# Local attention, then a squared-ReLU layer: four tiles to a group for the last eight tiles, and a new instruction order

## The chip, the cores and the metric

The kernel runs on one core of one Trainium2 chip. The metric is the device time in microseconds (us) of one execution; a number given for a version is the median of its runs. The profile is that of one execution, and its span is a little shorter than the device time.

## The reference

```python
scores = scale * np.matmul(q, k.transpose(0, 1, 3, 2))      # q, k, v: 4 x 8 x 768 x 64, float32
keep = is_global | is_local        # the first 8 keys, and the last 96 keys up to the query
scores = np.where(keep, scores + bias, -1000000000.0)       # bias: -slope of the head * distance
a = softmax(scores)
x = np.matmul(a, v)                # as 3072 tokens x 512
h = x @ w_in                       # 512 x 2048
r = np.maximum(h, 0.0)
out = (r * r) @ w_out              # 2048 x 512, float32
```

Each query sees at most 96 keys behind it and 8 at the start of its sequence. Most of the arithmetic is in the two products of the layer that follows.

## The kernel before

**Tiles.** The 3072 tokens are 24 tiles of 128, six to a sequence. Matmul inputs are bfloat16, sums float32.

**Attention of a tile.** GpSimd's queue (POOL) loads q, k and v, three DMAs a tile (line 213), converting them to bfloat16. q and k go into a ring of buffers (`qk_ring`, six for the first tiles and `NQ` = 3 for the later ones), v has a buffer for each tile. From tile 6 on, a DMA transpose on the SP queue (line 424) turns q and k into `qkT`. TensorE makes the scores (`sc`, line 487), ACT the exponentials (`exp`, line 553), DVE multiplies by mask and bias (`mul`, line 578), TensorE multiplies by v (`pv`, into the tile `po`, line 640), and DVE divides by the sum (`norm`, lines 667 and 668), giving `x`. From tile 8 on a DMA transpose (line 727) makes `xT` of it; before that TensorE does (`trx`, line 703). A score step may be joined to that of the tile before (`JOIN`), and then needs both tiles' `qkT`.

**The two products.** Two tiles form a block, 256 tokens. The first product `s1` (line 755) runs in eight units a block: each unit takes 256 of the 2048 hidden columns and is eight matmuls of 256 columns into one PSUM bank `hT` (128 x 512 float32). ACT applies the ReLU into `hr` (line 776), DVE squares it into `hs` (line 788), a ring of 14 buffers. The second product `s2` (line 828) takes `hs` as weights: two matmuls of 512 columns for each unit and tile, adding up over the eight units in `acc`, one PSUM bank for each tile of the block. ACT or DVE copies a finished bank to `o` (lines 328 and 330), and SP stores it (line 870). The last tile's sum is made in two pieces, of 384 and of 128 columns, the 128-column piece last.

**PSUM.** Eight banks: two for `acc`, six (tag `g`) shared by `hT`, `sc`, `po` and the transposes. An operation that takes a bank waits for the users of the bank's last tile.

**The order.** No engine picks its own order. A planner (`Plan`) gets each operation with a cost, its dependencies and a due time (`key`), plays the engines through, and always takes the operation with the smallest start plus a small multiple of its due time. The kernel then emits the instructions in that order, and each engine runs its own in order. `SHIFT` and `LEADS` move due times, `STEP` and `HOLD` tie a score step to a first-product unit, `SAFE` and `SAFEX` add a margin behind single transposes. `gate` is a small DVE write that holds back an early load.

Of the kernel before, what the change touches and what calls it, by code (L numbers as in the profile page):

```python
# [21 lines left out]
class Plan:  # L22
# [11 lines left out]
    SHIFT = {'T': 47, 'sc': -5.25, 'pv': -2, 'norm': 26.5, 'trx': -2, 'xT': 51, 'gk': 42, 'gv': -127.5, 'mul': 24, 'kl': 38.5, 'relu': 25.5, 'sq': 30, 's2': -5, 'o': 61, 'st': 78, ('mul', 3): 28, ('tr', 4): 10, ('xT', 5): -22, ('sc', 6): 14, ('pv', 7): -4, ('norm', 7): -17, ('trx', 7): -3, ('sc', 8): -12, ('pv', 8): -18, ('pv', 10): 45, ('sc', 11): 12, ('pv', 12): -50, ('sc', 13): 17, ('sc', 14): 6, ('pv', 14): 10, ('norm', 14): -28, ('sc', 15): -21, ('exp', 15): 20, ('exp', 16): 83, ('mul', 16): 92, ('norm', 16): -9, ('sc', 17): 32, ('pv', 17): 28, ('pv', 21): 9.5, ('pv', 22): -10, ('norm', 22): 8, ('s1', 2): -8.5, ('sq', 2): -10, ('relu', 3): 24, ('sq', 3): -82, ('s1', 5): 6, ('s1', 6): 30, ('sq', 6): 6, ('s1', 7): -6, ('sq', 7): -92, ('relu', 8): 40, ('s1', 9): -2, ('s1', 10): -10, ('s2', 0): 7.5, ('s2', 2): 1, ('s2', 4): -15, ('s2', 5): 37, ('s2', 6): -5, ('s2', 7): -3, ('s2', 9): 4.5, ('s2', 11): 30}  # L34
# [70 lines left out]
def kernel(  # L105
# [31 lines left out]
    NBLK = NT // 2  # L137
# [7 lines left out]
    NQ, NKT = 3, 2 * TPB  # L145
# [14 lines left out]
    v_sb = [const([P, H, VROW], BF16, f"v_{j}")[:, :, : D + 1] for j in range(NT)]  # L160
# [17 lines left out]
    LEADS = {3: 51, 4: 17, 5: 16, 6: 27, 8: 2, 9: 20, 10: 42, 11: 47, 12: 0, 14: 0, 15: 7.5, 16: 34, 17: 46, 20: 28, 21: 15, 23: 56}  # L178
# [6 lines left out]
    COPY = [14, 15, 19, 20, 22]  # L185
    BEHIND = {}
    HOLD = ((10, 0),)
    STEP = {(4, 0): -7, (12, 0): 37, (5, 0): -2, (10, 0): 29, (13, 0): 30, (23, 1): 81}
    JGATE = 11
    NHS = 14  # L190
    NWARM = 8
    NLATE, NO = 2, 4
    CUT = 3 * d_model // 4
    HALVES = ((NBLK - 3, 1), (NBLK - 2, 0), (NBLK - 2, 1))
# [9 lines left out]
    def slot(j):  # L204

        return j if j < NFIRST + 2 else NFIRST + 2 + j % NQ
# [14 lines left out]
    for j in range(NPLAIN):  # L221
        for n, src in ((0, q), (1, k)):
            t_ = const([P, d_model], FP32, f"plain_{n}{j}")
            nc.sync.dma_start(
                out=t_.rearrange("p (h d) -> p h d", h=H),
                in_=src_rows(src, j).rearrange("h p d -> p h d"),
            )
            plain[n, j] = t_
            land["qk"[n], j] = 4.1 + 1.1 * n
# [73 lines left out]
    for g in range(NFIRST + 2, NT, 6):  # L303
        js = range(g, min(g + 6, NT))
        o = plan.op(
            ("ones", g), {"DVE": 0.2}, lambda e, js=js: emit_ones(e, js),
            key=-1.0, ready=15.0,
        )
        ones.update({j: o for j in js})
# [41 lines left out]
    qk_users = [[] for _ in qk_ring]  # L351
    xT_op = {}
# [5 lines left out]
    for j in range(NT):  # L358
        b, t = divmod(j, TPB)
        first = t == 0  # L360
        need = 8 * (j // 2)
        base = need - LEADS.get(j, LEAD) + 4 * (j % 2)
# [4 lines left out]
        if j in late:  # L367
# [3 lines left out]
            if NFIRST + 2 + NQ - 1 <= j < JGATE:  # L371
# [10 lines left out]
                deps=qk_users[slot(j)] + [ones[j], gate], key=base, ready=issue[0],  # L382
            )
            qk_users[slot(j)] = []
            ld = plan.op(("data", j), {"DMAQ": 2.7}, None, deps=[ld])
# [36 lines left out]
        if j >= JQK:  # L422
            def emit_dT(e, j=j, T_=T_):
# [7 lines left out]
                deps=[land["q", j], land["k", j], xT_op[j - 3]] + ku, key=base - 6,  # L431
# [195 lines left out]
        for hf in range(2):  # L627
# [32 lines left out]
            users.append(p_)  # L660

# [21 lines left out]
        if 1 <= t < TPB - 1:  # L683
# [5 lines left out]
            )  # L689


        blk, tt = divmod(j, 2)
        if tt == 0:
            xT_users = []
        xT_ring = ("xT", 3, [xT_users]) if tt == 0 else None
        if j < JX:
# [16 lines left out]
            def emit_xT(e, j=j, blk=blk, tt=tt):  # L713
                if tt == 0:
                    tiles["xT", blk] = work.tile([P, KM, 2 * P], BF16, name="xT", tag="xT", bufs=3)
                any_copy(
                    e, tiles["xT", blk][:, :, tt * P : (tt + 1) * P], tiles.pop(("trx", j))
                )
# [4 lines left out]
        else:  # L723
            def emit_xT(e, j=j, blk=blk, tt=tt):
                if tt == 0:
                    tiles["xT", blk] = work.tile([P, KM, 2 * P], BF16, name="xT", tag="xT", bufs=3)
                nc.sync.dma_start_transpose(
                    out=tiles["xT", blk][:, :, tt * P : (tt + 1) * P],
                    in_=tiles["x", j].rearrange("p h d -> p (h d)"),
                )  # L730
# [9 lines left out]
        xT_of[blk] = xT_users  # L740
        if tt == 1:
            (xop if j >= JX else c)["deps"].append(xT_op[j - 1])


    order1 = [(blk, s) for blk in range(NBLK) for s in range(NSTEP)]
    square = {}
    s1_ops = {}
    for n, (blk, s) in enumerate(order1):
        users = []

        def emit_s1(e, blk=blk, s=s):
            hT = ps_g.tile([P, 2, 2 * P], FP32, name="hT", tag="g")
            for c in range(2):
                for kt in range(KM):
                    nc.tensor.matmul(  # L755
                        out=hT[:, c, :],
                        lhsT=w_in_sb[s][:, kt, c * P : (c + 1) * P],
                        rhs=tiles["xT", blk][:, kt, :],
                        start=(kt == 0),
                        stop=(kt == KM - 1),  # L760
                        skip_group_check=True,
                    )
            tiles["hT", blk, s] = hT

        a = plan.op(
            ("s1", blk, s), {"PE": 0.87}, emit_s1,
            deps=[xT_op[2 * blk], xT_op[2 * blk + 1], land["win", s]],
            key=float(n), takes=(*G, [users]),
        )
        s1_ops[blk, s] = a  # L770
        xT_of[blk].append(a)
        users.append(a)

        def emit_relu(e, blk=blk, s=s):
            hr = work.tile([P, 2, 2 * P], FP32, name="hr", tag="hr")
            nc.scalar.activation(hr, tiles.pop(("hT", blk, s)), Act.Relu)  # L776
            tiles["hr", blk, s] = hr

        rusers = []
        r = plan.op(("relu", blk, s), {"ACT": 0.48}, emit_relu, deps=[a], key=n + 0.5, takes=("hr", 2, [rusers]))  # L780
        users.append(r)
        rusers.append(r)
        husers = []

        def emit_sq(e, blk=blk, s=s):
            hs = work.tile([P, 2, 2 * P], BF16, name="hs", tag="hs", bufs=NHS)
            hr = tiles.pop(("hr", blk, s))
            nc.vector.tensor_mul(hs, hr, hr)  # L788
            tiles["hs", blk, s] = hs

        d = plan.op(("sq", blk, s), vec(0.61), emit_sq, deps=[r], key=n + 1.0, takes=("hs", NHS, [husers]))
        rusers.append(d)
        husers.append(d)
        square[blk, s] = (d, husers)

    for o in plan.ops:
        if o["name"][0] == "sc":
            j = o["name"][1]
            n = STEP.get(o["name"][1:], 4 * j - LEAD)
            if n >= 0 and j >= NFIRST:  # L800
                o["deps"].append(s1_ops[n // NSTEP, n % NSTEP])
                if o["name"][1:] in HOLD:
                    n += 1
                    s1_ops[n // NSTEP, n % NSTEP]["deps"].append(o)

    for blk in range(NBLK):
        last = blk == NBLK - 1
        acc_users = {}

        parts = [(0, None), (1, 0), (1, 1)] if last else [(0, None), (1, None)]  # L810
        order2 = (
            [(s, *p) for p in parts for s in range(NSTEP)]
            if last
            else [(s, *p) for s in range(NSTEP) for p in parts]
        )
        for s, sub, half in order2:
# [5 lines left out]
            def emit_s2(e, blk=blk, s=s, sub=sub, half=half, w=w, cols=cols, own=own):  # L822
                if s == 0:
                    pool, tag = (ps_g, "g") if own else (ps_acc, "acc")
                    tiles["acc", blk, sub, half] = pool.tile([P, w], FP32, name="acc", tag=tag)
                hs = tiles["hs", blk, s]
                for c in range(2):
                    nc.tensor.matmul(  # L828
                        out=tiles["acc", blk, sub, half],
                        lhsT=hs[:, c, sub * P : (sub + 1) * P],  # L830
                        rhs=w_out_sb[s][:, c, cols],
                        start=(s == 0 and c == 0),
                        stop=(s == NSTEP - 1 and c == 1),
# [3 lines left out]
            d, husers = square[blk, s]  # L837
            o = plan.op(
                ("s2", blk, s, sub), {"PE": 0.43 * w / d_model}, emit_s2,
                deps=[d, land["wout", s]] + users[-1:],  # L840
                key=8 * blk + s + 2.0 + (0 if not last else 8 * sub + 8 * (half or 0)),
# [4 lines left out]
            n = NSTEP * blk + s  # L846
            m = n + max([d for at, d in BEHIND.items() if n >= at], default=0)
            if m > n and m < NSTEP * NBLK:
                o["deps"].append(s1_ops[m // NSTEP, m % NSTEP])
            if s == NSTEP - 1:  # L850
# [70 lines left out]
```

## Time and profile before

| | us |
|---|---|
| device time, median of 3 runs | 211.02 (210.82 to 211.27) |
| span of the profile | 209.2 |
| TensorE (PE) busy | 202.4 |
| VectorE (DVE) busy | 141.4 |
| ScalarE (ACT) busy | 120.4 |
| GpSimd (POOL) busy | 74.0 |
| first product, 768 matmuls, busy | 93.3 |
| second product, busy | 87.1 |

PE is the matmul row and PEld the weight loads, which run beside the matmuls. The mean duration of a matmul in the groups (273 ns for 256 columns) includes its way through the array; when matmuls follow each other their starts are closer than that, so counts and stretches tell more than means. Some matmul records are missing from the trace, which looks like a short gap. The chain of waits goes back from the last instruction to what released each step.

### The profile page before, as it was taken

Reading aid. Unit: us, or ns where it says so; the run is one execution under the profiler, and the core shown is the slowest. Engines: PE = TensorE matmul, PEld = TensorE weight load, DVE = VectorE, ACT = ScalarE, POOL = GpSimd, SP = SyncE. Lnnn points to the kernel's source line nnn. Section 1 sums busy time; section 2 is a strip of 40 time slices with the busy share of each in tenths; the row PEclk is TensorE's granted clock in tenths of the full one; section 3 lists DMA queues with packets and bytes.
Section 4 is the critical chain, followed back from the end, with each engine's and each line's share of the span. In section 5 each row is a group of like instructions: output and inputs, shape, how many; then the busy total and the mean of one; then the engine's idle time right before and its main releaser. Section 6 shows DMA issues by size and latency. Waiting matters only on the chain.

```text
span 209.2 us, 4979 instructions
## 1 busy us (share of the span) xinstructions
PE 202.4 (97%) x1957; PEld 142.0 (68%) x1984; DVE 141.4 (68%) x370; ACT 120.4 (58%) x224; POOL 74.0 (35%) x91
## 2 busy tenths in 40 slices
PE   7989999999999999999999999999999999999994
PEld 3768887665756667676856676676676865865853
DVE  7698788533695788584958666676696865781730
ACT  6777688234872674655736564663575826841631
POOL 8997765541936086040545223122500000000000
PEclk9999999999999999999999999999999999999999
DMA  8999999999999999969799993979993421140402
GB/s 127 152 173 188 182 191 199 178 196 220 125 164 123 235 131 131 198 89 141 169 157 107 198 103 53 143 124 120 207 64 75 130 48 28 58 92 3 102 0 100
DMA packets 112664, 27.32 MB, mean 131 GB/s; under 512 B 103297, under 2 KB 109697, under 8 KB 112641
## 3 DMA queue, kind: packets, MB, share of 16 engines
q0 software_dynamic: 79200, 13.37, 84.8%
q1 hardware_dynamic: 33440, 13.64, 33.1%
q8 instruction: 15, 0.25, 0.5%
q14 instruction: 9, 0.07, 0.1%
HBM read 27.26 MB, written 6.29 MB: 160 GB/s over the span
## 4 chain that ended last, share of the span: by engine, by line
PE 88%; POOL 5%; DMA 3%; issue 1%; ACT 0%; POOLq 0%
PE acc L828 39%; PE hT L755 39%; PE sc L487 5%; PE po L640 4%; DMA win<-in_moe_w_in_dram 3%; POOL qk L213 3%; POOL v L213 2%; POOL win L213 1%; PE trx L703 1%; PE tr L400 1%; POOL pbi L267 0%; ACT o L328 0%; POOLq L267 0%; POOLq L902 0%
## 5 line engine op out<-in xcount | busy, mean ns | idle before, releaser
L755 PE MATMUL hT<-xT,win 128*128 128x256 bf16 x768 | 93.3, 273 | 0.7 <-DMA win<-in_moe_w_in_dram 0.6
L828 PE MATMUL acc<-wout,hs 128*128 128x512 bf16 (+2 forms) x373 | 87.1, 370 | 1.7 <-issue 0.3
L776 ACT ACTIVATE hr<-hT 128x512 f32<-128x512 f32 x96 | 57.4, 602 | 47.3 <-PE hT L755 41.5
L755 PEld LDWEIGHTS <-win 128*128 128x128 bf16 x768 | 72.9, 98 | 14.9 <-DMA win<-in_moe_w_in_dram 1.1
L788 DVE TENSOR_TENSOR hs<-hr 128x512 bf16<-128x512 f32 x96 | 64.8, 686 | 22.6 <-ACT hr L776 21.8
L828 PEld LDWEIGHTS <-hs 128*128 128x128 bf16 x400 | 36.8, 98 | 33.8
L553 ACT ACTIVATE esc<-sc 128x512 bf16<-128x512 f32 x78 | 39.9, 611 | 12.7 <-PE sc L487 12.6
L213 POOL DMA_DIRECT2D qk<-in_q_dram x23 | 20.7, 898 | 72.0 <-DMA qkT<-qk 55.9
L578 DVE TENSOR_TENSOR at<-esc,E 128x512 bf16<-128x512 bf16 x78 | 32.5, 424 | 10.3 <-ACT esc L553 7.5
L328 ACT COPY o<-acc 128x512 f32<-128x512 f32 (+2 forms) x21 | 11.6, 575 | 19.8 <-PE acc L828 19.8
L213 POOL DMA_DIRECT2D v<-in_v_dram x24 | 21.7, 904 | 1.4 <-DMA win<-in_moe_w_in_dram 1.0
L668 DVE TENSOR_TENSOR x<-po,rs 128x256 bf16<-128x256 f32 x48 | 20.4, 425 | 1.7
L213 POOL DMA_DIRECT2D qk<-in_k_dram x23 | 20.6, 895 | 0.5 <-DMA win<-in_moe_w_in_dram 0.5
L640 PEld LDWEIGHTS <-at 128*128 128x128 bf16 x352 | 15.7, 98 | 4.5
L640 PE MATMUL po<-v,at 128*128 128x65 bf16 x352 | 17.3, 193 | 0.0
L667 DVE RECIPROCAL rs<-po 128x4 f32<-128x4 f32 x48 | 8.5, 178 | 11.2 <-PE po L640 10.7
L487 PEld LDWEIGHTS <-qkT 64*128 64x128 bf16 x312 | 9.4, 94 | 5.9 <-issue 4.9
L487 PE MATMUL sc<-qkT 64*128 64x128 bf16 x192 | 12.6, 218 | 0.0
L487 PE MATMUL sc<-qkT,qkT 64*128 64x128 bf16 x120 | 8.5, 216 | 0.2 <-DVE rs L667 0.2
L330 DVE COPY o<-acc 128x512 f32<-128x512 f32 x4 | 2.8, 692 | 6.0 <-PE acc L828 6.0
L213 POOL DMA_DIRECT2D win<-in_moe_w_in_dram x8 | 6.1, 767 | 1.2 <-DMA win<-in_moe_w_in_dram 0.5
L213 POOL DMA_DIRECT2D wout<-in_moe_w_out_dram x8 | 5.7, 710 | 1.9 <-DMA win<-in_moe_w_in_dram 1.5
(45 smaller groups left out, 70.2 us busy)
## 6 DMA issues: line engine op xcount, KB each, us to landing
out_dram<-o SPq DMA_DIRECT2D x20, 256.0 KB, 3.2
v<-in_v_dram POOLq DMA_DIRECT2D x24, 128.0 KB, 5.8
qk<-in_q_dram POOLq DMA_DIRECT2D x23, 128.0 KB, 4.6
qk<-in_k_dram POOLq DMA_DIRECT2D x23, 128.0 KB, 5.2
win<-in_moe_w_in_dram POOLq DMA_DIRECT2D x8, 256.0 KB, 7.8
wout<-in_moe_w_out_dram POOLq DMA_DIRECT2D x8, 256.0 KB, 9.2
out_dram<-o SPq DMA_DIRECT2D x6, 128.0 KB, 2.4
qkT<-qk SPq DMA_TRANSPOSE x18, 4.8
```

Source lines behind the costliest of these rows:

```text
L213: nc.gpsimd.dma_start(out=dst, in_=src)
L328: nc.scalar.copy(dst, src)
L487: nc.tensor.matmul(out=tiles["sc", j, odd, g][:, at, :], lhsT=left[j - 1][half, pair, :] if kt else qkT[j % NKT][half, 1, pair, :], rhs=qk ...
L553: nc.scalar.activation(out=esc, in_=tiles.pop(("sc", j, odd, g)).rearrange("p a c -> p (a c)"), func=Act.Exp, scale=scale,)
L578: nc.vector.tensor_mul(at, tiles.pop(("esc", j, odd, g)), bias)
L640: nc.tensor.matmul(out=po[:, hi, :], lhsT=tiles["at", j, odd, g][:, at * P : (at + 1) * P], rhs=v_sb[kj][:, h, :], start=(i == 0), stop=(i ...
L667: nc.vector.reciprocal(rs, po[:, :, D : D + 1])
L668: nc.vector.tensor_tensor(out=x[:, 4 * hf : 4 * hf + 4, :], in0=po[:, :, :D], in1=rs.to_broadcast([P, 4, D]), op=Alu.mult,)
L755: nc.tensor.matmul(out=hT[:, c, :], lhsT=w_in_sb[s][:, kt, c * P : (c + 1) * P], rhs=tiles["xT", blk][:, kt, :], start=(kt == 0), stop=(kt ...
L776: nc.scalar.activation(hr, tiles.pop(("hT", blk, s)), Act.Relu)
L788: nc.vector.tensor_mul(hs, hr, hr)
L828: nc.tensor.matmul(out=tiles["acc", blk, sub, half], lhsT=hs[:, c, sub * P : (sub + 1) * P], rhs=w_out_sb[s][:, c, cols], start=(s == 0 an ...
```

## The change

Tiles 16 to 23 are worked in two groups of four tiles, 512 tokens, in place of four blocks of two. A first-product unit of such a group takes 128 hidden columns and is four matmuls of 512 columns into the same bank; there are 16 units. With two `acc` banks, the second product of a group makes two passes over the hidden columns: tiles 0 and 1 of the group, then tiles 2 and 3. In the last group the last tile is again cut into 384 and 128 columns. The purpose is fewer and wider matmuls and fewer weight loads in the first product.

Around it: `hs` becomes a ring of eight larger buffers, four units each; `xT` buffers hold four tiles; v gets a ring of 12 buffers, so that a load waits for the last reader of the tile 12 before; the q/k ring has four late buffers; six `o` buffers, the first two lent to the plain q and k of tile 0; `HOLD`, `STEP`, `LEADS` and `SHIFT` are new throughout, from a search over orders.

```diff
-    NBLK = NT // 2
+    QUADS = 16
+    GROUPS = [(j, 2) for j in range(0, QUADS, 2)] + [(j, 4) for j in range(QUADS, NT, 4)]
...
-    NQ, NKT = 3, 2 * TPB
+    NQ, NKT, NV = 4, 2 * TPB, 12
...
-    v_sb = [const([P, H, VROW], BF16, f"v_{j}")[:, :, : D + 1] for j in range(NT)]
+    v_ring = [const([P, H, VROW], BF16, f"v_{j}")[:, :, : D + 1] for j in range(NV)]
+    v_sb = {j: v_ring[j % NV] for j in range(NT)}
...
-    COPY = [14, 15, 19, 20, 22]
-    BEHIND = {}
-    HOLD = ((10, 0),)
-    STEP = {(4, 0): -7, (12, 0): 37, (5, 0): -2, (10, 0): 29, (13, 0): 30, (23, 1): 81}
+    COPY = sorted(j - 1 for j, _ in JOIN if j % TPB)
+    HOLD = ((15, 1), (17, 0), (19, 0))
+    STEP = {(14, 0): 36, (15, 1): 53, (17, 0): 46, (19, 0): 58, (20, 1): 62, (23, 1): 79, (4, 0): -7, (7, 0): 5, (13, 0): 32}
...
-    NHS = 14
+    NHS = 8
...
-    NLATE, NO = 2, 4
+    NLATE, NO = 2, 6
...
-                deps=qk_users[slot(j)] + [ones[j], gate], key=base, ready=issue[0],
+                deps=qk_users[slot(j)] + v_users[j % NV] + [ones.get(j % NV), gate], key=base, ready=issue[0],
...
-                deps=[land["q", j], land["k", j], xT_op[j - 3]] + ku, key=base - 6,
+                deps=[land["q", j], land["k", j], xT_op[j - (3 if j < QUADS - 2 else 6)]] + ku, key=base - 6,
...
-            hT = ps_g.tile([P, 2, 2 * P], FP32, name="hT", tag="g")
-            for c in range(2):
-                for kt in range(KM):
-                    nc.tensor.matmul(
-                        out=hT[:, c, :],
-                        lhsT=w_in_sb[s][:, kt, c * P : (c + 1) * P],
-                        rhs=tiles["xT", blk][:, kt, :],
...
+                hT = ps_g.tile([P, 4 * P], FP32, name="hT", tag="g")
+                nch = 4 // nt
+                for c in range(nch):
+                    ch = nch * s + c
+                    for kt in range(KM):
+                        nc.tensor.matmul(
+                            out=hT[:, c * nt * P : (c + 1) * nt * P],
+                            lhsT=w_in_sb[ch // 2][:, kt, (ch % 2) * P : (ch % 2 + 1) * P],
+                            rhs=tiles["xT", g][:, kt, :],
...
+        if nt == 4:
+            parts = [(2, None), (3, 0), (3, 1)] if last else [(2, None), (3, None)]
+            order2 = [(s, sub, None, n0 + 8.0 + s / 2) for s in range(nstep) for sub in (0, 1)]
+            if last:
+                order2 += [
+                    (s, sub, half, n0 + 16.0 + 8 * i + s / 2)
+                    for i, (sub, half) in enumerate(parts) for s in range(nstep)
+                ]
+            else:
+                order2 += [(s, sub, None, n0 + 16.0 + s / 2) for s in range(nstep) for sub in (2, 3)]
```

## The prediction

> **What bounds the kernel now.** I read the page's busy lines first, then the chain that ended last, then TensorE's waits, then the chain in order of time at both ends.
>
> ```profile
> span 209.2 us, 4979 instructions
> PE 202.4 (97%) x1957; PEld 142.0 (68%) x1984; DVE 141.4 (68%) x370; ACT 120.4 (58%) x224; POOL 74.0 (35%) x91
> PEclk9999999999999999999999999999999999999999
> DMA  8999999999999999969799993979993421140402
> ...
> PE 88%; POOL 5%; DMA 3%; issue 1%; ACT 0%; POOLq 0%
> ```
>
> TensorE is busy 97% at full clock, and 88% of the chain is TensorE; the other engines are far off. The second thing to see is the DMA line: nines until about 80 us and again around 105 to 125 us. Data arrives just in time, so DMA is the next bound behind TensorE. Does TensorE ever wait?
>
> ```profile
> PE warm L273 <- DVE zero L261: 1.2, 1, 1.2
> PE hT L755 <- DMA win<-in_moe_w_in_dram: 0.6, 2, 0.4
> PE acc L828 <- issue: 0.3, 2, 0.2
> PE acc L828 <- DVE hs L788: 0.3, 2, 0.2
> PE sc L487 <- DVE rs L667: 0.2, 1, 0.2
> ```
>
> Hardly: 2.6 us in all, most of it before the first product starts. The chain in order of time shows the two ends (start, us, what):
>
> ```profile
> 12.52 7.23 DMA win<-in_moe_w_in_dram
> 19.80 1.92 PE hT L755 x16
> ...
> 186.40 6.04 PE acc L828 x28
> 192.44 6.99 PE hT L755 x64
> ...
> 199.48 6.91 PE acc L828 x47
> 206.38 0.02 issue
> 206.41 0.27 ACT o L328
> ```
>
> Until 19.8 us the input weights set the pace; from 19.8 to 206.4 us TensorE has one piece after the other; then comes a tail of 2.8 us (evict, store, end). So only three things can move the time: the sum of TensorE's work after 19.8 us, new waits in it, and the tail.
>
> **What the Trainium skill says.** "TensorE: Matmul & The Clock Gate", section "Wait — 56ns, not 53.3ns?": a warm matmul starts every N/2.4 ns plus a fixed 2.5 ns or so, N being the columns. The trace agrees: 6.99 us / 64 = 109.2 ns for 256 columns (256/2.4 = 106.7), and 6.04 / 28 = 215.7 ns for 512 (213.3). The same page's "Back-to-back issue gap" gives 131 ns a matmul as a sustained rate at 512 columns; this trace does not agree, so I use 215.7. "DMA: Bandwidth & Descriptors", section "Issuing engines are not separate DMA queues": DMAs issued from different engines share the same 16 DMA engines and interleave. In the trace loads from POOL, transposes and stores from SP fall in the same nines.
>
> **Part 1: 512 columns a matmul (tiles 16 to 23).** 8 of 24 tiles change, so 256 of the 768 first-product matmuls become 128 of twice the width. Removed: 256 x 109.2 = 27.96 us. Added: 128 x 215.7 = 27.61 us. Gain 0.35 us, all on the path. It is that small because only the fixed 2.5 ns of 128 matmuls goes; the array streams the same columns. The 128 weight loads removed (98 ns each) overlap the matmuls (weight loads fill 68%) and cost nothing either way. Relu, square, evictions and second-product matmuls keep count and size.
>
> **Part 2: second product in two passes, groups of four.** The built program shows the order of each engine, which the planner sets. In TensorE's new order the 16 first-product units of a group stand in a row, then tiles 0 and 1 of the group accumulate, then 2 and 3. Can ACT and DVE keep up with 16 units? The stretch of 8 units at the end of before shows it:
>
> ```profile
> 192.44:199.42 6.98, 6.98 (x64) 6.20 (x64) 5.05 (x8) 4.37 (x8) 0.00 (x0) 1.00 0.35 76
> ```
>
> The columns are PE, weight loads, DVE, ACT and POOL. DVE needs 5.05 and ACT 4.37 us of 6.98, so both drain faster than TensorE fills, and 16 units behave like 8. I added up the trace's durations along the new order, without waits (an estimate): from the end of a first-product unit to the first second-product matmul that needs it there are now at least 3.6 us; in before the smallest distance was 1.7 us and cost nothing. So these waits have more room than before. Cost 0.
>
> **Part 3: the order, and what it asks of DMA.** Everything before the fourth first-product unit (19.8 us) is the same set of work behind the same weight load, so the start stays. After that attention runs earlier, because a group of four needs its four tiles whole. By the same sum, the scores of tile 13 come due at about 90 us (96.6 in before), of 14 at 97 (108.6), 17 at 119 (134.4), 19 at 134 (149.9), 22 at 163 (174.0). The loads must follow, through a DMA already at nines. Against that, the q/k ring goes from three slots to four, the gate before tile 8's load goes, and stores move back.
>
> The tight spots. (a) Tile 8 is now loaded before tile 7, which its scores need first (tile 7's stand joined with tile 6's, due at 53.1 us). A load takes POOL 3 x 0.9 = 2.7 us (0.898, 0.895 and 0.904 us an issue); tile 7's transpose landed at 49.3 us in before, so now near 52: 1 us of room. (b) The first product of tiles 8 and 9 is due at 76.8 us (80.1); tile 9's pv ends at 70.3, norm 2 x (0.18 + 0.43) = 1.2, the transpose's issue 1.2, landing 2.3 to 4.1 us later: 75.0 to 76.8, 0 to 2 us of room. (c) Tile 13's transpose waits on SP behind tile 10's (about 80 us) and lands near 87, due at 90. All hold, none with much to spare. What stands behind a late one: SP and TensorE are in order, so later transposes wait too, and every TensorE instruction after it slips by the full delay. I take 0.05 us for all this and keep 0 to 2 us.
>
> The v ring of 12 makes a load wait for the pv step 11 tiles back, tens of us before: 0. Fewer ones-memsets (12 x 65 ns) and one more kl copy (0.28 + 0.27 us) lie on a DVE that is 68% busy: 0.
>
> **Part 4: the tail.** In before the last accumulation is 128 columns wide; in the new order the 128-column piece goes ahead of the third tile's, and the last is the 384-column piece. TensorE's sum is the same, but what follows is longer: copy 0.48 against 0.27 us (ACT's timeline), store 1.9 against 1.6 us to landing (the DMA issues; KB, us).
>
> ```profile
> 205.51 0.48 ACT L328 COPY o<-acc 128x384 f32<-128x384 f32 x1 [2.01 <-PE acc L828]
> 206.41 0.27 ACT L328 COPY o<-acc 128x128 f32<-128x128 f32 x1 [0.41 <-PE acc L828]
> ```
>
> ```profile
> out_dram<-o SPq DMA_DIRECT2D x1, 192.0 KB, 1.9
> out_dram<-o SPq DMA_DIRECT2D x1, 64.0 KB, 1.6
> ```
>
> That costs 0.21 + 0.3 = 0.5 us, hidden by nothing. The third tile's first matmul also needs tile 0's bank: 0.22 + 16 x 0.056 + 0.17 = 1.3 us of room for 0.28 + 0.59 + 0.2 = 1.1: holds.
>
> **Sum.** 211.02 - 0.35 + 0.5 + 0.05 = 211.2 us. The change leaves the bound where it is, takes 0.35 us off it, and gives that back at the end.
>
> **Rivals.** (1) A transfer comes late and TensorE gains a wait. For it: DMA at nines, attention 12 to 16 us earlier in the middle, the three spots. Against it: one more ring slot, fewer stores ahead, and every spot holds in my sums. One or two late transfers of 0.5 to 1 us: 211.8 to 212.7, say 212.0 us. (2) The new order is smoother than I price it and the tail costs less: the waits of 0.3 + 0.3 us on the second product go, the 0.35 comes off, half the tail penalty is hidden: 211.02 - 0.35 - 0.6 + 0.25 = 210.3 us, faster. Against it: TensorE was saturated, so there is next to nothing left to gain, and some of those small waits are gaps where a matmul record is missing. (3) ACT or DVE falls behind in the two long first-product stretches, by 0.05 us on each of 32 units: 1.6 us, 212.8 us. The stage table above speaks against it.
>
> **From this to the numbers.** No difference 0.48 (211.2); a late transfer 0.30 and a slow engine 0.05, together slower 0.35; faster 0.17. The threshold of 0.2% is 0.42 us. The range runs from rival 2 with a margin less (210.4) to two late transfers of 1 us each (213.0).
>
> **What would show it.** In the changed kernel's profile: 128 matmuls of hT at 128x512 of about 216 ns each when back to back; TensorE's chain unbroken from 19.8 us to about 206.1; the last ACT copy 128x384 at 0.48 us, 2.8 + 0.5 us between TensorE's end and the span's end. A wait of TensorE for qkT or xT of over 0.4 us, near 53, 77 or 90 us, would show rival 1; a chain that ends near 205.4 us would show rival 2. I am wrong in the mechanism if the 512-column matmuls take clearly less than 216 ns.

## The result, and the profile after

The changed kernel takes 213.82 us (median of 6 executions, 212.86 to 214.14), the kernel before 211.17 us beside it (6 executions): 2.65 us slower, ratio 1.0115 with a 95% interval of 1.009 to 1.014. The prediction was 211.2 us; the time lies beyond its range of 210.4 to 213.0. A later series gave 214.43 against 211.68 us, 2.75 us slower. Medians from here on leave out executions in a slower state of the chip, those over 1.5% above the fastest of the same kernel.

The page of the changed kernel, the lines that were shown of before:

```profile
span 212.1 us, 4750 instructions
PE 203.2 (96%) x1832; PEld 128.8 (61%) x1856; DVE 142.0 (67%) x360; ACT 121.1 (57%) x223; POOL 73.8 (35%) x91
PEclk9999999999999999999999999999999999999999
DMA  9999999999999999999999999751110025400032
...
PE 48%; DMA 35%; POOL 7%; DVE 5%; issue 2%; ACT 1%; SPq 0%; ACTq 0%; POOLq 0%; DVEq 0%
```

TensorE's busy time and clock are nearly as before, but the chain has changed hands: TensorE's share fell from 88 to 48%, DMA's rose from 3 to 35%. The DMA line has nines without a gap up to some 130 us, where before has a six at 89 us, a seven at 99 us and a three at 125 us. About 34 of DMA's 74 us in the chain lie before 48.6 us, on loads of the weights and of tile 7's k; the three places below lie after that. The chain in order of time (start, us, what) shows three of the places where a transfer ended a wait of TensorE:

```profile
48.60 6.06 DMA qkT<-qk
54.66 0.05 issue
54.70 0.62 PE sc L492 x16
...
84.13 8.35 DMA qkT<-qk
92.48 0.05 issue
92.53 0.62 PE sc L492 x16
...
96.64 8.71 DMA xT<-x
105.35 0.03 issue
...
105.44 0.42 DVE x L676
```

Read each as: issued, so long under way, then TensorE (or DVE, which then holds TensorE up) goes on at once. The transpose of tile 7 landed at 54.66 us, that of tile 13 at 92.48 us, and the norm of tile 14 waited until 105.35 us for one of the two x buffers, which the transpose of tile 12 was still reading. The table of TensorE's waits has 0.7 us for the scores and little else, too little for 2.9 us. I therefore laid the durations of the trace along TensorE's order without waits, as for the prediction, and took the lag of the trace behind that sum:

| lag gained | first execution, us | second execution, us |
|---|---|---|
| up to 20 us (weights) | 1.07 | 0.41 |
| 55 us, scores of tiles 6 and 7 | 0.32 | 1.04 |
| 92 us, scores of tile 13 | 0.80 | 0.92 |
| 108 us, first product of tiles 12 and 13 | 0.47 | 0.56 |
| 128 us, pv of tile 17 | 0.23 | 0.17 |
| 169 us, scores of tile 23 | 0.13 | 0.13 |
| total, with smaller steps | 3.14 | 3.40 |

The sums of this table are mine, not a view; the waits at 92 us (0.73 and 0.85 us) and, in the second execution, at 55 us (0.86 us) stand in the timelines too. The first row is the start, which differs from execution to execution. To these come the longer tail (+0.44) and the width (-0.35). The sum without waits also leaves out some 0.3 us of small waits that before had: 3.14 + 0.44 - 0.35 - 0.3 = 2.9 us, the difference of the spans (212.1 - 209.2).

Why is the DMA late? The transfers issued between 50 and 128 us, before and then after (count, KB, median us from issue to landing):

```profile
out_dram<-o SPq DMA_DIRECT2D x10, 256.0 KB, 3.7
qk<-in_q_dram POOLq DMA_DIRECT2D x12, 128.0 KB, 4.0
qk<-in_k_dram POOLq DMA_DIRECT2D x12, 128.0 KB, 5.0
v<-in_v_dram POOLq DMA_DIRECT2D x12, 128.0 KB, 5.4
qkT<-qk SPq DMA_TRANSPOSE x11, 5.4
xT<-x SPq DMA_TRANSPOSE x8, 3.6
```

```profile
out_dram<-o SPq DMA_DIRECT2D x9, 256.0 KB, 5.3
qk<-in_q_dram POOLq DMA_DIRECT2D x15, 128.0 KB, 6.8
qk<-in_k_dram POOLq DMA_DIRECT2D x15, 128.0 KB, 7.0
v<-in_v_dram POOLq DMA_DIRECT2D x15, 128.0 KB, 7.5
qkT<-qk SPq DMA_TRANSPOSE x15, 7.1
xT<-x SPq DMA_TRANSPOSE x9, 6.8
```

In the same 78 us the DMA now has three more tiles to load, four more q/k transposes and one more x transpose, against one store less. Every kind takes 1.6 to 3.2 us longer to land.

The end, in the timeline of the changed kernel:

```profile
206.27 0.59 ACT L330 COPY o<-acc 128x512 f32<-128x512 f32 x1 [3.19 <-PE acc L864]
...
208.87 0.48 ACT L330 COPY o<-acc 128x384 f32<-128x384 f32 x1 [2.01 <-PE acc L864]
```

The last copy is the 384-column one, 0.48 us; from TensorE's end (208.84 us) to the end of the span are 3.26 us, 2.82 before.

### The profile page after: what moved, and what is told of

Read it like the earlier page. It is cut to its first block, busy times and chain, and to the rows that moved or that the text cites. A ratio compares the mean times of both kernels' runs of the same rounds, so it can differ in the third digit from the quotient of the medians.

```text
span 212.1 us, 4750 instructions
## 1 busy us (share of the span) xinstructions
PE 203.2 (96%) x1832; PEld 128.8 (61%) x1856; DVE 142.0 (67%) x360; ACT 121.1 (57%) x223; POOL 73.8 (35%) x91
## 4 chain that ended last, share of the span: by engine, by line
PE 48%; DMA 35%; POOL 7%; DVE 5%; issue 2%; ACT 1%; SPq 0%; ACTq 0%; POOLq 0%; DVEq 0%
PE acc L864 25%; PE hT L770 18%; DMA qkT<-qk 13%; DMA wout<-in_moe_w_out_dram 9%; DMA xT<-x 4%; DMA win<-in_moe_w_in_dram 4%; POOL qk L215 4%; DMA qk<-in_k_dram 3%; DVE hs L807 3%; PE po L645 3%; PE sc L492 2%; DMA v<-in_v_dram 2%; POOL v L215 2%; POOL win L215 1%; DVE x L676 1%
## 5 line engine op out<-in xcount | busy, mean ns | idle before, releaser
L770 PE MATMUL hT<-xT,win 128*128 128x256 bf16 (+1 forms) x637 | 89.1, 293 | 1.5 <-DMA win<-in_moe_w_in_dram 1.2
L770 PEld LDWEIGHTS <-win 128*128 128x128 bf16 x640 | 61.0, 98 | 24.4 <-DMA win<-in_moe_w_in_dram 2.1
L864 PEld LDWEIGHTS <-hs 128*128 128x128 bf16 x400 | 36.2, 98 | 35.3
L558 ACT ACTIVATE esc<-sc 128x512 bf16<-128x512 f32 x78 | 40.5, 607 | 17.4 <-PE sc L492 14.6
L583 DVE TENSOR_TENSOR at<-esc,E 128x512 bf16<-128x512 bf16 x78 | 31.3, 421 | 5.7 <-ACT esc L558 3.7
L330 ACT COPY o<-acc 128x512 f32<-128x512 f32 (+2 forms) x22 | 12.5, 575 | 25.5 <-PE acc L864 25.5
L645 PE MATMUL po<-v,at 128*128 128x65 bf16 x352 | 17.8, 193 | 0.5 <-ACT at L558 0.2
L332 DVE COPY o<-acc 128x512 f32<-128x512 f32 x3 | 2.1, 692 | 11.2 <-PE acc L864 11.2
L492 PE MATMUL sc<-qkT,qkT 64*128 64x128 bf16 x112 | 8.0, 216 | 0.0
```

Source lines behind the costliest of these rows:

```text
L330: nc.scalar.copy(dst, src)
L492: nc.tensor.matmul(out=tiles["sc", j, odd, g][:, at, :], lhsT=left[j - 1][half, pair, :] if kt else qkT[j % NKT][half, 1, pair, :], rhs=qk ...
L558: nc.scalar.activation(out=esc, in_=tiles.pop(("sc", j, odd, g)).rearrange("p a c -> p (a c)"), func=Act.Exp, scale=scale,)
L583: nc.vector.tensor_mul(at, tiles.pop(("esc", j, odd, g)), bias)
L645: nc.tensor.matmul(out=po[:, hi, :], lhsT=tiles["at", j, odd, g][:, at * P : (at + 1) * P], rhs=v_sb[kj][:, h, :], start=(i == 0), stop=(i ...
L770: nc.tensor.matmul(out=hT[:, c * nt * P : (c + 1) * nt * P], lhsT=w_in_sb[ch // 2][:, kt, (ch % 2) * P : (ch % 2 + 1) * P], rhs=tiles["xT" ...
```

## The experiments

Theory A: the groups themselves cost nothing; the order asks for attention earlier than a full DMA can bring it, and TensorE waits for late transfers; to this comes the tail. Theory B: groups of four cost TensorE time by themselves (two passes, drains, PSUM banks). Times are medians; the difference is to the kernel before in the same series (211.2 to 211.7 us), unless another partner is named. All edits but those named "before" are on the changed kernel.

### Does any of it stay when nothing is late?

First the v loads alone were left out, in both kernels, from tile 6 on (the expectation says 8, which is wrong; tiles 6 and 7 are in it). These tiles then multiply by an earlier tile's v:

```diff
...
         load_part(0, j)
         load_part(1, j)
-        load_v(j)
+        if j < NFIRST + 2:
+            load_v(j)
```

> The changed kernel with the v loads of tiles 8 to 23 left out: these tiles multiply by the v of an earlier tile. The order of all other instructions is kept. A third of the late load traffic is gone. To be read against the same edit in the kernel before (next run). Theory A (what the change costs is transposes and loads that come late on a DMA that is full): with the DMA relieved the difference to the kernel before with the same edit falls from 2.65 us to what is left of tail and width, 0.44 - 0.35 = 0.1 us, at most 0.6 us; waits of TensorE for qkT and xT under 0.5 us in all. Theory B (four tiles to a group cost TensorE time by themselves: two passes, drains, PSUM banks): the difference stays at 1.5 us or more.

> The kernel before with the v loads of tiles 8 to 23 left out in the same way. It waits hardly at all for data as it is (2.6 us of waits, most of it before 20 us), so both theories expect 210.3 to 211.2 us: at most 0.7 us less than the kernel before.

Measured: 212.66 and 211.29 us, 1.37 us apart. Neither theory's number. The trace says why: one wait was left, and it is a transfer.

```profile
91.83 0.23 PE L497 MATMUL sc<-qkT 64*128 64x128 bf16 x2 [1.05 <-DMA qkT<-qk]
```

The transpose of tile 13 took 8.9 us to land; four loads of q and k, issued at 79.6 to 82.2 us just ahead of it, were under way beside it. So the same, with tile 13's transpose moved ahead of tile 14's and the 128-column piece last:

> The changed kernel with the v loads of tiles 8 to 23 left out, as two runs ago, and also the transpose of tile 13 ahead of that of tile 14 and the 128-column piece last. With the v loads alone left out, the profile had one wait of TensorE for a transpose left, 1.0 us for tile 13, and the longer tail. Theory A (late transfers, and the tail): both go, and what remains is the gain of the wide matmuls: 211.29 - 0.35 = 210.9 us, at most 211.6 us. Theory B (the groups cost TensorE time by themselves): 212.0 us or more.

Measured: 212.14 us, ratio to the kernel before 1.0021 (1.000 to 1.0043). Theory A's 210.9 is missed again; in its trace the norm of tile 14 waited until 104 us for the x buffer that the transpose of tile 12 still read, TensorE lost some 0.5 us by it at 108 us, and the start was 0.6 us late. Then all late loads went, in both kernels:

> The changed kernel with all loads of q, k and v of tiles 6 to 23 left out: these tiles use the q, k and v of an earlier tile. All transposes, stores and the work of the engines stay, in the same order. Leaving out v alone still left a wait for the transpose of tile 13, because loads and transposes still shared the DMA. Theory A (what the change costs, tail apart, are transfers that come late): nothing on the DMA is late any more, and the difference to the same edit in the kernel before (next run) is -0.35 + 0.44 = 0.1 us, at most 0.5 us. Theory B (the groups cost TensorE time by themselves): 1.2 us or more.

> The kernel before with the loads of tiles 6 to 23 left out in the same way. Both theories: it waited hardly for them, so 210.3 to 211.3 us.

Measured: 214.29 and 211.27 us. The 3 us looked like theory B, but they lie at the start: with nothing to wait for, the transpose of tile 6 was issued at 10.33 us, among the weights, and landed at 19.33 us. TensorE waited several times between 16 and 22 us and had a granted clock of 0.55 from 22 to 25 us. From the TensorE transpose for tile 4 (at 25.24 us here, at 21.91 us in the kernel before with this edit) to its end it took 184.5 us, against 184.8: nothing is lost there. With the loads of tiles 6 and 7 back, and those from tile 8 on left out:

```diff
...
-        load_part(0, j)
-        load_part(1, j)
-        load_v(j)
+        if j < JX:
+            load_part(0, j)
+            load_part(1, j)
+            load_v(j)
...
-                    in_=qk_ring[slot(j)].rearrange("p n c -> p (n c)"),
+                    in_=qk_ring[slot(j) if j < JX else 1 + j % (TPB - 1)].rearrange("p n c -> p (n c)"),
```

> The changed kernel with the loads of q, k and v of tiles 8 to 23 left out (these tiles use an earlier tile's). With the loads of tiles 6 and 7 left out too, the transpose of tile 6 had nothing to wait for, was issued at 10.3 us and delayed the weights by 2 us at the start: now it waits for its load again. Theory A: 0.1 us above the same edit in the kernel before (next run), at most 0.5 us, and no wait of TensorE for a transpose after 20 us. Theory B: 1.2 us or more above it.

> The kernel before with the loads of tiles 8 to 23 left out in the same way: 210.3 to 211.5 us for both theories.

Measured: 211.31 (14 executions) and 211.30 us (21): no difference, where theory A said 0.1 and theory B 1.2 or more. The page of the changed kernel with this edit:

```profile
DMA  9999999994261567539292375251110035400032
...
PE 88%; POOL 5%; DMA 3%; issue 1%; ACT 0%; POOLq 0%
```

The shares of the chain are those of before, while grouping, passes and order are those of the change. The traces say it without scatter. In the kernel before and in its three variants (without v, and without the loads from tile 6 or from tile 8 on) it is 186.6 us each time from the start of the fourth first-product unit to TensorE's end. In the chain of this run it is 198.42 + 7.55 - 19.71 = 186.3 us, 0.3 less, which is the forecast gain of the width with no wait added:

```profile
19.71 1.92 PE hT L775 x16
...
198.42 7.55 PE acc L869 x50
```

The changed kernel takes 188.0 and 188.9 us there in its two traces. The longer tail gives back 0.44. Theory B falls; what the change costs needs a DMA that is busy with loads.

### One late transfer at a time

The transpose of tile 13 ahead of that of tile 14, in the finished order:

```diff
-    for o in plan.run({"PE": 4.2, "DVE": 4.2, "ACT": 5.3, "DMAQ": issue[1]}):
+    order = plan.run({"PE": 4.2, "DVE": 4.2, "ACT": 5.3, "DMAQ": issue[1]})
...
+    move(("T", 13), ("T", 14))
+    for o in order:
```

> The changed kernel with one move on the SP queue: the transpose of tile 13 ahead of that of tile 14. Theory A: tile 13 lands before its scores are due and the 0.8 us wait near 92 us goes: 213.0, or somewhat above where a later transpose takes its place. Theory B: no difference, 213.8.

Measured: 213.16 us, 1.51 above before, 1.14 less than the change cost. The six executions reach from 212.10 to 214.56 us, so the time alone doesn't decide. The trace does for tile 13: its transpose landed at 88.71 us and the wait at 92 us was gone. But in this trace, of the fastest execution, the wait at 55 us was gone too, which the edit doesn't touch (tile 7's transpose landed at 53.47 us), the weights came 1.0 us earlier, and the scores of tile 10 waited 0.3 us at 74 us. So part of the 1.14 us is scatter. Then five moves at once, the fifth being the 128-column piece last (its code stands under the tail below):

```diff
...
+    move(("load", 7), ("load", 8))
+    move(("load", 10), ("load", 12))
+    move(("T", 13), ("T", 14))
+    for name in (("T", 16), ("st", 3, 0), ("st", 3, 1)):
+        move(name, ("T", 17))
...
```

> The changed kernel with five moves in the finished order: load 7 ahead of load 8, load 10 ahead of load 12 (its gate dropped), transpose of tile 13 ahead of that of tile 14, transpose of tile 16 and the two stores of tile pair 6 and 7 behind the x transposes of tiles 12 and 13, and the 128-column piece of the last tile last. Theory A: the waits at 55, 74, 92 and 107 us go (0.32 + 0.35 + 0.80 + 0.4 us) and the tail is 2.8 us again (0.44): 2.65 - 2.3 = 0.3 us above the kernel before, 0 to 0.8 us. Theory B, or moves that only push the delay to the next transpose: 1.2 us or more above it.

Measured: 212.32 us (212.50 over all 22 executions, the number that the next expectations use), ratio 1.0034 (1.0011 to 1.0056), 0.81 above before: at the upper edge of theory A's 0 to 0.8. The waits at 55, 92, 108 and 128 us were gone from its trace (the one at 74 us that the expectation names was in the trace of the run before, not in that of the changed kernel). A new one had come, of 0.76 us at 98 us (chain):

```profile
91.14 6.30 DMA xT<-x
97.45 0.03 issue
...
97.54 0.42 DVE x L676
```

DVE, and with it TensorE's next score step, waited until the transpose of tile 11 had read its x buffer, which the norm of tile 13 needed. There were two x buffers; a third was added, and by mistake of mine tile 15's transpose was moved back too:

> The changed kernel with the five moves, and also a third x buffer (in the profile of the five moves the norm of tile 13 waited for the x buffer that the transpose of tile 11 was still reading: its landing took 6.3 us, TensorE lost 0.76 us) and the transpose of tile 15 behind the x transposes of tiles 11 and 12. Theory A: the last wait goes, 0.7 us less than with the five moves: 211.8 us, within 0.3 us of the kernel before. If each mended wait is followed by another elsewhere, because the DMA as a whole is too late between 80 and 125 us, it stays at 212.3 us or more.

Measured: 220.37 us. The scores of tile 15 are joined with those of tile 14, due at 97 us; I had taken tile 15 to be due at 114. TensorE waited 7.7 us for it, and then ran on a reduced clock (each line: stretch, its length in us, PE busy with matmuls, granted clock, DMA, GB/s):

```profile
98.50:106.50 8.00, 0.68 (x17) 0.84 2.07 135
106.50:109.50 3.00, 2.58 (x13) 0.50 0.86 211
109.50:112.50 3.00, 3.00 (x28) 0.80 0.88 181
112.50:115.50 3.00, 3.00 (x36) 1.00 1.76 181
```

Without that mistake, the five moves and a third x buffer:

```diff
...
-                    tiles["x", j] = work.tile([P, H, D], BF16, name="x", tag="x")
+                    tiles["x", j] = work.tile([P, H, D], BF16, name="x", tag="x", bufs=3)
```

> The changed kernel with the five moves and a third x buffer, the transpose of tile 15 back in its place (its scores are joined with those of tile 14, due at 97 us: moving it back cost 7.7 us of wait in the run before). Theory A with single late transfers: the wait of 0.76 us at 98 us goes, about 0.5 us less than the 212.5 us of the five moves: 212.0 us. If the DMA as a whole is late between 80 and 125 us, another transfer is late in its place and it stays at 212.3 us or more.

Measured: 211.83 us, ratio 1.0029 (1.0005 to 1.0054), 0.38 above before. Theory A's 212.0 holds: of the 2.65 us all but 0.4 is back (0.44 of what is back is the tail). Its profiled execution was its fastest, 210.59 us. There TensorE waited for nothing after 20 us; the last lines of its chain:

```profile
172.48 5.83 PE acc L864 x27
178.30 13.81 PE hT L770 x64
192.12 13.87 PE acc L864 x80
```

TensorE ended at 205.97 us, 0.40 us before it does in the kernel before; 0.22 us of that is a fourth weight that landed earlier (19.53 against 19.75 us). But its executions reach from 210.59 to 213.73 us with a standard deviation of 1.1 us, where before in that series has 0.5. Perhaps the scatter of the DMA becomes waiting time on a schedule without room; that isn't shown, as only the fastest execution was traced. It does not beat the kernel before.

### Tail, width, stores

The tile order of the last pass changed to tiles 0, 1, 2, the 384 and last the 128-column piece:

```diff
...
+    tail = [o for o in order if o["name"][0] in ("s2", "o", "st") and o["name"][1] == last]
+    tail.sort(key=lambda o: (min(o["name"][-1], 2), o["n"]))
+    order = [o for o in order if all(o is not x for x in tail)] + tail
...
```

> The changed kernel with the last group's second product in the order tile 0, tile 1, tile 2, the 384-column piece of tile 3, the 128-column piece last. If the longer tail (copy of 384 in place of 128 columns, larger store) is worth 0.44 us: 213.4. If the tail hides behind something else: 213.8.

Measured: 213.67 us, 2.02 above before, 0.63 less than the change. The executions reach from 212.24 to 213.86 us and can't tell 213.4 from 213.8. The trace can: from TensorE's end to the end of the span are 2.80 us, as in before (2.82), where the changed kernel has 3.26. The end of its timeline:

```profile
208.43 0.48 ACT L330 COPY o<-acc 128x384 f32<-128x384 f32 x1 [2.01 <-DMA out_dram<-o]
209.33 0.27 ACT L330 COPY o<-acc 128x128 f32<-128x128 f32 x1 [0.41 <-PE acc L864]
```

The 512-column matmuls cut into two of 256:

```diff
...
-                    for kt in range(KM):
+                    for p, kt in [(p, kt) for p in range(nt // 2) for kt in range(KM)]:
...
-                            rhs=tiles["xT", g][:, kt, :],
+                            rhs=tiles["xT", g][:, kt, 2 * p * P : (2 * p + 2) * P],
```

> The changed kernel with each 512-column matmul of the first product as two of 256 columns, each with its own weight load, same order otherwise. If the width saves what the fixed cost of a matmul says (128 x 2.7 ns): 0.35 us slower, 214.2, all of it after 150 us. If the wide form itself has a cost of its own: no difference or faster.

Measured: 214.98 us, 3.33 above before, 0.68 more than the change. Its waits for late transposes were larger too (2.5 us in its trace), so the time doesn't measure the width. That is read from its chain:

```profile
181.17 13.97 PE hT L770 x128
```

13.97 us / 128 = 109.1 ns, against 13.81 / 64 = 215.8 ns: 0.16 us a group, 0.32 us for two groups (the second group was measured, the first is taken to be like it); the prediction had 0.35.

The stores of tiles 0 to 9 left out, to empty the DMA:

```diff
...
-                    for r in range(0, P, n):
+                    for r in range(0, P if j >= 10 else 0, n):
```

> The changed kernel without the output stores of tiles 0 to 9 (ten stores of 256 KB left out, so those output rows are not written); every other instruction and the order of each engine stay. Theory A (late data: the transposes of q, k and x land after TensorE wants them because the DMA engines are full from 45 to 125 us): the waits near 55, 92, 108 and 127 us, together about 1.8 us, mostly go: 211.8 to 212.5. Theory B (the new order itself costs TensorE, by grouping, evictions or engine waits): 213.5 to 214.0, as the changed kernel.

Measured: 214.39 us, 2.74 above before: nothing gained. In its trace, which is that of the slowest of its six executions, the transpose of tile 13 landed later still, at 93.72 us. It took 10.5 us to land. Three loads that the changed kernel issued at 83.8 to 85.6 us were issued here at 82.3 to 84.1 us, around this transpose's own issue at 83.24 us. That they ran ahead because the stores were gone, and that this made the transpose later, is likely, but one trace doesn't show it.

```profile
93.76 0.29 PE L492 MATMUL sc<-qkT 64*128 64x128 bf16 x2 [2.80 <-DMA qkT<-qk]
...
94.73 2.47 PE L864 MATMUL acc<-wout,hs 128*128 128x512 bf16 x6
```

### Why did the order let them be late?

The planner takes a q/k transpose for 1.2 us of DMA time and a store for 1.4 us. The DMA by itself:

> Measures the DMA by itself; the whole computation is left out, only loads, transposes and stores of the kernel's sizes run, each kind alone in a burst and then beside loads. From the traces so far: a load part 0.87 us of DMA time, a q/k transpose 1.9 us, an x transpose 1.0 us, a store of 256 KB 0.7 to 0.8 us. The planner's prices are 0.9, 1.2, 0.9 and 1.4 us. Theory A expects the transposes in a burst to land about 1.9 us apart and the stores under 1 us apart; if transposes land 1.2 to 1.3 us apart, as fast as SP issues them, the price was right and the delay comes from something else.

Measured. Alone, six transposes landed 1.35 us apart on average, as fast as SP issued them, so the burst doesn't show the expected 1.9 us: it is the expectation's other case; x transposes landed 1.3 us apart, also as issued; stores 0.67 us apart, loads 0.85. Beside loads it is different. The transposes alone, then loads and transposes together, then stores and transposes together (issues: count, KB, median us to landing):

```profile
qkT<-qk SPq DMA_TRANSPOSE x6, 3.3
```

```profile
v<-in_q_dram POOLq DMA_DIRECT2D x6, 128.0 KB, 7.9
v<-in_k_dram POOLq DMA_DIRECT2D x6, 128.0 KB, 7.6
v<-in_v_dram POOLq DMA_DIRECT2D x6, 128.0 KB, 7.9
qkT<-qk SPq DMA_TRANSPOSE x6, 6.4
```

```profile
out_dram<-o SPq DMA_DIRECT2D x6, 256.0 KB, 2.7
qkT<-qk SPq DMA_TRANSPOSE x6, 3.3
```

The 6.4 us is the median of six, two of which landed before the first load did; the four among the loads took 5.5 to 9.6 us. Beside stores the transposes take 3.3 us as alone: stores don't hinder them here, which speaks for the loads as what makes them late, and fits that leaving out the stores gained nothing.

From 50.6 us (two transposes landed) to the last landing at 73.28 us passed 22.7 us with 18 loads and four transposes: 22.7 - 18 x 0.85 = 7.4 us, 1.85 us for each of the four (an estimate: it holds the transposes for the only other cost). With 1.9, 1.0 and 0.8 us as prices, a new order was made (the search also set all margins of `SAFE` and `SAFEX` to zero):

> The changed kernel with an order found anew, after the planner's DMA prices were set to what the traces show: 1.9 us for a q/k transpose in place of 1.2, 1.0 for an x transpose, 0.8 for a store in place of 1.4; due times, ties and margins are new. A third x buffer, and the 128-column piece last. Theory A with the DMA prices as the reason why the order came out too tight: its transfers are on time, so it gets the gain of the wide matmuls: 211.3 - 0.35 = 211.0 us, 210.7 to 211.6. If the prices are not the reason (it is the sharing of the DMA by transfers in flight at the same time, which a price for each cannot say), late transfers remain and it stays at 212 us or more.

> The same, and the transpose of tile 13 ahead of that of tile 14. If tile 13 is still late in the new order, 0.3 to 0.8 us less than the run before; if it is on time there, the same.

Measured: 218.01 us (ratio 1.030), and for the second 218.92 and 219.94 us in the two executions that count (ratio 1.035, 1.031 to 1.040). Both are worse than the change, and the second is slower than the first, where its expectation said the same or less. The first waited 3.0 us at 69 us for a transpose, and had a granted clock of 0.70 and 0.73 in the six us after it:

```profile
68.75 0.23 PE L492 MATMUL sc<-qkT 64*128 64x128 bf16 x2 [2.96 <-DMA qkT<-qk]
```

So new prices alone didn't mend the order. As due times, ties and margins changed with them, the run doesn't tell which of these made it slower, and whether the prices were the reason stays open. The planner serves transfers one after the other; in the run above those in flight share the DMA (loads took 4.7 us to land alone and 7.6 to 7.9 us beside transposes), and a price for each can't say that. A planner with sharing was not tried.

### The changed kernel again

> The changed kernel itself once more. In its first profile the fourth input weight landed at 20.82 us, 1.07 us later than in the profile of the kernel before; in the profiles of its variants it landed between 19.56 and 21.02 us. If that is chance, it lands at another time here, near 20 us, the waits for the transposes of tiles 7 and 13 are there again, and the median is 213 to 214 us. If the start of this program is late by itself, it lands at 20.8 us again.

Measured: 214.43 us, 2.75 above before. The fourth weight landed at 20.17 us. The start differs from execution to execution, but it is not paid twice: lag at the start and at 55 us together is 1.39 and 1.45 us in the two executions. The transpose of tile 7 landed at 54.66 and 54.73 us, and that sets the time of the scores in both, wherever TensorE was before.

```profile
54.77 0.23 PE L492 MATMUL sc<-qkT 64*128 64x128 bf16 x2 [0.86 <-DMA qkT<-qk]
92.74 0.23 PE L492 MATMUL sc<-qkT 64*128 64x128 bf16 x2 [0.85 <-DMA qkT<-qk]
```

## Why the prediction was wrong

**Part 1, width: right.** 0.35 us predicted, 0.32 read from the chains.

**Part 2, two passes and the engines at no cost: right.** Without the loads from tile 8 on the changed kernel takes the same time as before with the same edit (211.31 and 211.30 us); its TensorE is 0.3 us faster by the width, and no wait for DVE's squares is on its chain. Rival 3 didn't happen.

**Part 3, order and DMA at 0.05 us: this is the step that failed.** The text named the right spots and then said "All hold, none with much to spare". Spot (a), the transpose of tile 7 "now near 52", due at 53.1, landed at 54.66 us. It was issued 3.8 us later than in before (48.60 against 44.76 us, where 2.7 were counted) and took 6.1 us to land in place of 4.5. Spot (c), tile 13 "lands near 87, due at 90", landed at 92.48 us. The text doesn't name the transpose of tile 14, which stands ahead of it on SP; and it took 8.4 us to land, 6.2 us in before. Moved ahead of tile 14's, it landed at 88.71 us. Spot (b), the x transpose of tile 9, held by luck: it landed at 77.07 us, after the 76.8 us at which it was due, but TensorE was 1.4 us late by then and came to it at 78.29 us. A fourth, the x buffer of tile 14 behind the transpose of tile 12, was not seen. In place of 0.05 us TensorE lost 1.4 us up to 55 us, 0.8 at 92 and 0.5 at 108 (first execution).

What (a) and (c) share is the time to land, taken too close to the emptier profile of before. Its DMA line was read as emptier than it is, too: the nines reach to 89 us, not to about 80, so tile 13's transpose falls in a full stretch. The sum over all transfers was not made. The counts for it stand in the order: three tiles of loads, four q/k transposes and one x transpose more, one store less in 78 us are 3 x 2.6 + 4 x 1.85 + 1.0 - 0.7 = 15.5 us of DMA time more, on a DMA that already had nines for most of that stretch. (This is an estimate: the 1.85 is from the DMA run, made afterwards, and the 1.0 for an x transpose is assumed.) That the sum, and not the place of single transfers in the queues, is what makes them late is argued, not shown. The Trainium skill has a mechanism for it in "DMA: Bandwidth & Descriptors", section "Queues, rings and completion order": each DMA engine goes round the queues that have work for it, packet by packet. No run here shows these turns; the runs agree so far as a transpose doesn't go ahead of loads that are under way, 3.3 us alone and 5.5 to 9.6 us among loads. The fourth q/k buffer, which the prediction counted as a help, lets more of those loads be under way; whether three buffers would have been better was not tried.

**Part 4, tail +0.5: right,** 0.44 in the trace, and gone again in the trace with the 128-column piece last.

**Start: right in kind.** It is set by the weights and varies between executions (fourth weight at 20.82 and 20.17 us), and does not add to the wait at 55 us.

**The rivals.** Rival 1, a late transfer, is what happened, at a chance of 0.30 and 212.0 us; it counted on one or two late transfers, there are four, and the tail comes on top.

## What to carry to other kernels

When a change pulls work forward, add up the DMA time of everything that must now be issued in each stretch and set it against the free DMA time of that stretch, before looking at single transfers; landing times read from a profile with an emptier DMA don't carry over. (No order made by such a sum was tried here.) One late transfer mended shows the next one, so room has to be made for all of them: here five moves, one of them for the tail, and one more buffer gave back 2.3 of 2.65 us. An experiment that empties one kind of traffic may not help the transfer that is late: with the v loads left out tile 13's transpose landed at 91.79 us, with stores left out at 93.72, in place of 92.48. So look at which traffic hinders it, and at what the queues do with the room. And where executions scatter by 1 us, measure a stretch in the traces: 186.6 against 186.3 us showed what the medians could not.

## What the runs showed of the hardware

A long wait of TensorE costs more than its length. After 2.80 us of waiting (stores left out) the granted clock was 0.53 for the next 3.3 us: the scores and the six matmuls behind them took 3.3 us, and 1.9 us in the changed kernel, where the clock was 1.00. After 2.96 us (new prices) it was 0.70 and 0.73 in the six us that followed, after 7.74 us it was 0.50 for 3 us and 0.80 for 3 more. Single waits of 1.6 us and less left it at 1.00. Several short ones together did not: with the loads from tile 6 on left out, TensorE was busy for 3.6 of 6 us with no wait over 1.34 us, and had 0.55 in the 3 us after. The Trainium skill, "TensorE: Matmul & The Clock Gate", section "What's actually happening", gives an idle window of about 3.4 us for the drop; here less was enough.

A DMA transpose of 256 KB between SBUF buffers and the loads hinder each other: alone the transpose landed after 3.3 us, beside stores after 3.3 us too, among loads after 5.5 to 9.6 us, and took some 1.85 us of DMA time each (an estimate from 22.7 us for 18 loads and four transposes).
